# Softmax exponentials in mid phase, first-tile convolution terms summed on VectorE, conversions gated by their own loads

## The chip, the cores and the metric

One core of one Trainium2 chip runs the kernel as one program. The metric is device microseconds of one execution, lower is better. TensorE (PE) does the matmuls, VectorE (DVE) and ScalarE (ACT) the elementwise work, SyncE's queue (SP) issues the DMAs, and GpSimd (POOL) does almost nothing.

## What is computed

A causal convolution of 7 taps with softmax weights per head, then two feed-forward layers, in fp32, over 2 x 4096 tokens of 192 channels.

```
w = softmax(weight_gen, axis=-1)            # [2, 4096, 8 heads, 7 taps]
out[s, h, :] = sum_k w[s, h, k] * x_pad[s + k, h, :]     # 6 rows of zeros ahead, 24 channels a head
x = out.reshape(8192, 192)
x = (silu(x @ w_gate) * (x @ w_val)) @ w_out             # moe:  192 -> 1536 -> 192
h = x @ w_in                                             # moe2: 192 -> 2048 -> 192
result = (h * clip(h + 3, 0, 6) / 6) @ w_out2
```

## The kernel before

**Tiles and phases.** The 8192 tokens are 16 tiles of 512. A tile goes through the convolution, the first layer M1 (phase (1,t), 12 blocks of 128 of the 1536 columns) and the second layer M2 (phase (2,t), 8 blocks of a pair of 128 columns each). Tiles 0 and 1 go through M1 interleaved, as `START` says (so many blocks of tile 0, then so many of tile 1 and tile 0 by turns). Then come phases (1,2), (1,3), and from there (2,t) and (1,t+3) alternate.

**A product in fp32.** Every operand is split into a rounded high part (fp32r, a Copy on ScalarE) and the rest (a subtraction on VectorE), and a product is three passes on TensorE over half heights of 64 rows (L604, L763, L685). An M1 block is: projections pg and pv (L604), Silu on ScalarE (L638), product (L641, DVE), high part gh (L617, ACT), low part gl (L646, DVE), output matmuls (L685). An M2 block is: two projections ph (L604, 18 records), two Relu with bias 3 (L724, ACT), min and product (L728, DVE), gh (L617), gl (L736), output matmuls (L763). The `ph` tiles sit in four PSUM buffers, so the projections of block k+2 need the L728 of block k. In TensorE's order the 12 last matmuls of one block's projections and the 6 first of the next can stand side by side, with output matmuls behind them.

**Boundaries between layers.** At the start of (2,t) the sums of M1 are split on ScalarE and VectorE into M2's operand (L702, L703, L704, L705, L659, L660); this chain is named y below. M2's output matmuls (L763) write PSUM banks that the chain reads, so they wait for it.

**The convolution.** Softmax weights are made for two tiles at a time in items: peak (L325), subtraction (L328), Exp on ScalarE (L329), total (L332), L336, reciprocal (L337), scale (L340). Exp and Silu lie in different function tables of ScalarE, so each change costs an ACT_TABLE_LOAD; Relu and Copy need none. From tile 2 on, taps (L360) and their sums (L385) run on VectorE. For tiles 0 and 1 each of the 7 taps (`conv_pe_items`) goes as a product on VectorE (`tmp`, L360) and as a term of transposing matmuls on TensorE (L421, 16 records in the trace), which adds up the 7 terms in PSUM; `transposes` then has the sum split (L469, L471 on ACT, L475, L477 on DVE). `heat` issues matmuls of no use between (L452).

**Weights.** The weights come as 64-bit words (raw) and are taken apart into fp32 by an exponent on ScalarE (L212), three steps on VectorE (L218, L221, L227), and the split (L278, L296 on ACT, L263 on DVE).

**What sets the order.** The order on each engine is planned when the program is built: `V["A"]` and `V["D"]` are modelled times of ScalarE and VectorE, `fill` takes items of the convolution (queue c) and of the weights (queue w) with a due block (`dues`) into gaps. ScalarE's work that items ask for goes into `late_act`, and `run_act` issues it when the model has room; `urgent` holds the splits that the next phase needs.

Of the kernel before, what the change touches and what calls it, by code (L numbers as in the profile page):

```python
# [38 lines left out]
def conv_swiglu_relu6_kernel(  # L39
# [11 lines left out]
    nc = tc.nc  # L51
# [19 lines left out]
    START = [(0, 6), (6, 10), (10, 12)]  # L71
# [52 lines left out]
    def load_x(t):  # L124
# [12 lines left out]
        def before():  # L137
            for b in range(B):
                r0 = (b * PB + 1) * J - z
                nc.sync.dma_start(  # L140
                    out=xt[b * PB + 1:(b + 1) * PB, :z, :],
                    in_=xf[r0:r0 + (PB - 1) * J, :].rearrange("(p j) d -> p j d", j=J)[:, :z, :],
                )
# [5 lines left out]
    late_act, late_pe, urgent = [], [], []  # L149
# [18 lines left out]

    def run_urgent():
        run_act()  # L170
        while urgent:
            f, a, d, ready = urgent.pop(0)
            f()
            on("A", a, ready)
            on("D", d, ready + min(a, 700.0))

# [6 lines left out]
    def load_raw(limit):  # L183
        while loaded[0] < min(limit, len(chunks)):
# [13 lines left out]
    def convert_stream(q0, q1):  # L198
# [9 lines left out]
        def exponent(q):  # L208
# [6 lines left out]
            late_act.append((gates["e", q], go, chunks[q][0] + 110, V["D"]))  # L215
# [90 lines left out]
    def softmax_items(t0, t1):  # L306
# [97 lines left out]
    def conv_pe_items(t):  # L404

        n = sizes[t]

        def tap(k):
            def go():
                src = vp if k % 2 else pools["c"]  # L410
                o = src.tile([P, MJ, D], F32, tag="tmp", name="tmp", bufs=2)
                taps(nc.vector, t, k, o)
                if k == 0:
                    after_taps(t)

                def pe():
                    if k == PAD:
                        pe_t[t] = [acc_bank(0), acc_bank(2)[:D2]]
                    for dst, a, b in zip(pe_t[t], (0, P), (P, D)):
                        for s in range(n):  # L420
                            nc.tensor.matmul(  # L421
                                dst[:, s * P:(s + 1) * P], o[:, s, a:b], ident,
                                start=k == PAD and s == 0, stop=k == 0 and s == n - 1,
                            )
                late_pe.append((pe, V["D"]))
            return go

        return [(v_cost(n * D), tap(k)) for k in range(PAD, -1, -1)]
# [25 lines left out]
    def run_pe(limit=None):  # L454
        while late_pe and (limit is None or late_pe[0][1] <= limit):
            f, ready = late_pe.pop(0)
            f()
            clock[:] = [max(clock + [ready]) + 1150] * 2

    def transposes(t, banks=None):  # L460
# [5 lines left out]
        if t in pe_t:  # L466
# [5 lines left out]
            late_act.append(([False], rounds, 1850, max(clock) + 300))  # L472

            def lower():
                nc.vector.tensor_sub(s0[:, 1, :N], ba, s0[:, 0, :N].bitcast(F32))  # L475
                for r in HALVES:
                    nc.vector.tensor_sub(s2[r, 1, :N], bb, s2[r, 0, :N].bitcast(F32))  # L477
                x_at[t] = max(V["D"] + 1900, V["A"])
            urgent.append((lower, 0, 1900, max(clock) + 600))
# [35 lines left out]
        late_act.append(([False], rounds, 1300, max(clock) + 600))  # L515

        def lower():
            for v, h, l in parts:
# [5 lines left out]
            x_at[t] = V["D"] + 4500  # L524
        urgent.append((lower, 0, 1500, max(clock) + 800))
# [191 lines left out]
    def m2_ew(b, t, i, ps, there):  # L717
# [15 lines left out]
        at = [on("A", 635, a) for a in at]  # L733
        fill(at[0], at[1] + 1000)
# [97 lines left out]
    def pop(q):  # L832
        at = ready(q)
        if at is None:
            run_act()
            at = ready(q)
# [173 lines left out]
    dues["c", 1] = START[0][1]  # L1010
# [20 lines left out]
    with tc.manual_schedule():  # L1031
# [13 lines left out]
        load_raw(2)  # L1045
        load_x(1)()
        load_raw(4)
        load_wg(1)
# [10 lines left out]
        first = taps0[:1] + s1[:2] + taps0[1:2] + s1[2:] + taps0[2:]  # L1059
# [72 lines left out]
```

## Time and profile before

| | |
|---|---|
| time, median of 3 runs | 1294.22 us (1293.24 to 1295.1) |
| profiled execution | 1291.2 us, its span 1289.3 us |
| TensorE busy | 1259.3 us, 98% of the span |
| VectorE busy | 918.3 us, 71% |
| ScalarE busy | 679.5 us, 53% |
| mean granted TensorE clock | 0.991 of full speed |

The span is the time between the first and the last instruction of the trace; 1.9 us of the execution lie around it. A matmul that waits within the array or runs at a lower clock counts as busy.

### The profile page before, as it was taken

How to read it: one execution, taken by the hardware profiler on the slowest of the kernel's cores; microseconds unless marked ns; L12 is line 12 of the kernel's file. 1: busy time of each engine (PE TensorE's matmuls, PEld its weight loads, DVE VectorE, ACT ScalarE, POOL GpSimd, SP SyncE). 2: the span in 40 equal slices, each digit the busy share in tenths (PEclk: the TensorE clock that was granted, in tenths of full speed). 3: DMA queues.
4: the chain of work that ended last, by engine and by line, in shares of the span. 5: the costliest groups of instructions: out<-in, count | busy, mean ns of one | idle time of the engine just before them, and what ended most of it. 6: DMA issues, size and time to landing. Idle time of an engine off the chain costs nothing.

```text
span 1289.3 us, 29299 instructions
## 1 busy us (share of the span) xinstructions
PE 1259.3 (98%) x12176; PEld 1178.2 (91%) x12176; DVE 918.3 (71%) x1469; ACT 679.5 (53%) x1177; POOL 3.6 (0%) x11
## 2 busy tenths in 40 slices
PE   9889999999999999999999999999999999999998
PEld 7667978898899998999988999889989999999997
DVE  6779986887685947768586775859568594655665
ACT  3355564664554645555464545545455463645655
POOL 1000000000000000000000000000000000000000
PEclk9999999999999999999999999999999999999999
DMA  8312240011010100101001010010100000000000
GB/s 243 122 32 88 60 128 3 10 52 52 17 45 9 48 14 17 44 18 51 10 10 44 18 51 10 9 44 18 44 18 14 10 10 14 18 13 10 13 14 13
DMA packets 26580, 46.95 MB, mean 36 GB/s; under 512 B 3028, under 2 KB 19410, under 8 KB 26448
## 3 DMA queue, kind: packets, MB, share of 16 engines
q1 hardware_dynamic: 26448, 45.09, 12.0%
q8 instruction: 95, 1.56, 0.5%
q14 instruction: 37, 0.30, 0.1%
HBM read 30.92 MB, written 6.29 MB: 29 GB/s over the span
## 4 chain that ended last, share of the span: by engine, by line
PE 80%; DVE 9%; ACT 4%; issue 1%; DMA 0%; SPq 0%; ACTq 0%; DVEq 0%
PE a L763 21%; PE ph L604 19%; PE pv L604 14%; PE a L685 13%; PE pg L604 12%; DVE p L641 2%; ACT gh L617 1%; DVE gl L646 1%; DVE p L728 1%; ACT p L638 1%; DVE s L704 0%; ACT s L659 0%; DVE y L705 0%; DVE tmp L360 0%; DVE f L221 0%
## 5 line engine op out<-in xcount | busy, mean ns | idle before, releaser
L604 PE MATMUL pv<-s,wi 64*128 64x512 f32 x1728 | 449.0, 395 | 5.1 <-ACT p L638 3.8
L604 PE MATMUL pg<-s,wi 64*128 64x512 f32 x1728 | 427.6, 395 | 4.0 <-DVE wi L263 1.3
L617 ACT ACTIVATE gh<-p 128x512 fp32r<-128x512 f32 x448 | 279.0, 633 | 203.7 <-DVE p L641 161.1
L604 PE MATMUL ph<-s,wi 64*128 64x512 f32 x2304 | 330.1, 397 | 9.8 <-DVE p L728 9.1
L604 PEld LDWEIGHTS pv<-s,wi 64*128 64x128 f32 x1728 | 308.8, 184 | 26.6 <-ACT p L638 4.7
L763 PE MATMUL a<-wo,gh 64*128 64x384 f32 x2016 | 318.8, 357 | 1.4 <-DVE y L705 1.0
L604 PEld LDWEIGHTS pg<-s,wi 64*128 64x128 f32 x1728 | 297.8, 185 | 20.6 <-DVE wi L263 2.2
L763 PE MATMUL a<-wo,gl 64*128 64x192 f32 x2016 | 304.7, 250 | 0.0
L763 PEld LDWEIGHTS a<-wo,gh 64*128 64x128 f32 x2016 | 284.5, 187 | 6.0 <-DVE y L705 2.5
L604 PEld LDWEIGHTS ph<-s,wi 64*128 64x128 f32 x2304 | 263.6, 185 | 24.1 <-DVE p L728 14.7
L763 PEld LDWEIGHTS a<-wo,gl 64*128 64x128 f32 x2016 | 280.6, 190 | 0.1
L685 PE MATMUL a<-gh,wo 64*128 64x512 f32 x1152 | 254.9, 393 | 2.2 <-ACT wo L296 2.1
L724 ACT ACTIVATE p<-ph,three 128x512 f32<-128x512 f32 x256 | 162.2, 686 | 162.9 <-PE ph L604 162.6
L641 DVE TENSOR_TENSOR p<-p,pv 128x512 f32<-128x512 f32 x192 | 131.7, 686 | 131.4 <-ACT p L638 130.7
L685 PE MATMUL a<-gl,wo 64*128 64x512 f32 x768 | 212.3, 393 | 0.0
L728 DVE SCALAR_TENSOR_TENSOR p<-p,ph 128x512 f32<-128x512 f32 x256 | 164.0, 682 | 60.2 <-ACT p L724 59.9
L646 DVE TENSOR_TENSOR gl<-p,gh 128x512 fp32r<-128x512 f32 x192 | 132.7, 691 | 104.1 <-ACT gh L617 104.1
L638 ACT ACTIVATE p<-pg 128x512 f32<-128x512 f32 x192 | 114.7, 597 | 168.0 <-PE pg L604 141.7
L685 PEld LDWEIGHTS a<-gh,wo 64*128 64x128 f32 x1152 | 170.8, 184 | 12.3 <-ACT wo L296 2.6
L736 DVE TENSOR_TENSOR gl<-p,gh 128x512 fp32r<-128x512 f32 x256 | 165.6, 689 | 13.0
L685 PEld LDWEIGHTS a<-gl,wo 64*128 64x128 f32 x768 | 121.0, 185 | 6.2
L360 DVE TENSOR_TENSOR tmp<-xt,wg 128x768 f32<-128x768 f32 x98 | 92.5, 953 | 2.3 <-DMA xt<-in_x_dram 1.4
(65 smaller groups left out, 517.3 us busy)
## 6 DMA issues: line engine op xcount, KB each, us to landing
xt<-in_x_dram SPq DMA_DIRECT2D x14, 960.0 KB, 4.8
out_dram<-o SPq DMA_DIRECT2D x15, 384.0 KB, 2.3
s<-s SPq DMA_DIRECT2D x16, 256.0 KB, 2.8
s<-s SPq DMA_DIRECT2D x56, 64.0 KB, 2.0
raw<-in_moe_w_out_dram SPq DMA_DIRECT2D x8, 384.0 KB, 3.1
raw<-in_moe_w_out_dram SPq DMA_DIRECT2D x3, 768.0 KB
raw<-in_moe_w_in_dram SPq DMA_DIRECT2D x16, 128.0 KB, 2.3
wg<-in_weight_gen_dram SPq DMA_DIRECT2D x7, 224.0 KB, 5.0
```

Of the source, the lines that this page charges most:

```text
L360: eng.tensor_mul(o.rearrange("p j (h g) -> p j h g", h=H), xt_t[t][:, a + k:b + k, :].rearrange("p j (h g) -> p j h g", h=H), wg_t[t][:, a ...
L604: return nc.tensor.matmul(ps[b][:, :N], w[rows, s, m, c], x[rows, l, :N], start=start, stop=stop)
L617: nc.scalar.activation(gh[:, :N], p[:, :N], AF.Copy)
L638: nc.scalar.activation(p[:, :N], pg[:, :N], AF.Silu)
L641: nc.vector.tensor_mul(p[:, :N], p[:, :N], pv[:, :N])
L646: nc.vector.tensor_sub(gl[:, :N], p[:, :N], gh[:, :N].bitcast(F32))
L685: return nc.tensor.matmul(y[:, :N], wo1[rows, i, col:col + P], x[rows, :N], start=start, stop=stop)
L724: nc.scalar.activation(q, ph[:, :N], AF.Relu, bias=three)
L728: nc.vector.scalar_tensor_tensor(out=q, in0=q, scalar=6.0, in1=ph[:, :N], op0=ALU.min, op1=ALU.mult)
L736: nc.vector.tensor_sub(gl[:, :N], q, gh[:, :N].bitcast(F32))
L763: return nc.tensor.matmul(z[s][:, :w], x[rows, s * P:(s + 1) * P], late["wo2"][rows, blk, :w], start=start, stop=stop,)
```

## The change

Seven edits:

- **Exp.** The softmax's Exp goes into a list of its own, `late_exp`, which `run_exp` issues. In M2 it is called from the third block of a phase on. For tiles 2 and 3 peak, subtraction and Exp move ahead of the first Silu.
- **Terms.** `TERMS` groups the taps of tiles 0 and 1: taps of one group are added on VectorE (L440 of the changed kernel), and each group is one term on TensorE: 5 terms for tile 0 and 4 for tile 1, instead of 7 and 7.
- **START** goes from (0,6), (6,10), (10,12) to (0,4), (4,8), (8,12).
- **Loads.** `land["w", q]` gives a conversion its own load's modelled time. The second part of tile 0's x comes in 4 DMAs instead of 2, and the second load of softmax weights (`load_wg(1)`) stands ahead of tile 1's x.
- **Transposes.** The ACT half of the split of a tile's convolution (`rounds`) stands with its DVE half in `urgent`; `run_urgent` no longer calls `run_act` first.
- **Dues** of the softmax items of tiles 1 to 3 and the model's cost of a term (2100 for 1150).
- **End.** The last two blocks' output matmuls of the last tile: the first block's for all four strips of 128 tokens, and then the last block's strip by strip, instead of both blocks' strip by strip.

```diff
-    START = [(0, 6), (6, 10), (10, 12)]
+    TERMS = [[[6], [5], [4], [3, 2], [1, 0]], [[6, 5], [4, 3], [2, 1], [0]]]
+    START = [(0, 4), (4, 8), (8, 12)]
...
-            for b in range(B):
+            cuts = [z, z // 2, 0] if t == 0 else [z, 0]
+            for hi, lo in zip(cuts, cuts[1:]):
+                for b in range(B):
...
+    def run_exp():
+        while late_exp:
+            gate, f, ready = late_exp.pop(0)
+            f()
+            gate[0] = on("A", 1900, ready)
+
     def run_urgent():
-        run_act()
         while urgent:
...
+            land["w", q] = V["D"] + 5500
...
-            late_act.append((gates["e", q], go, chunks[q][0] + 110, V["D"]))
+            late_act.append((gates["e", q], go, chunks[q][0] + 110, max(V["D"], land["w", q])))
...
-            late_act.append((gate, lambda: nc.scalar.activation(w(), w(), AF.Exp), 3100, V["D"]))
+            late_exp.append((gate, lambda: nc.scalar.activation(w(), w(), AF.Exp), V["D"]))
...
+        def add():
+            o = box["tmp"][:, :n, :]
+            nc.vector.tensor_add(o, o, box["acc"][:, :n, :])
...
+        for q, term in enumerate(TERMS[t]):
+            items.append((c, step(term[0], "tmp")))
+            for k in term[1:]:
+                items += [(c, step(k, "acc")), (c, add)]
...
-            late_act.append(([False], rounds, 1850, max(clock) + 300))
 
             def lower():
+                rounds()
...
         at = [on("A", 635, a) for a in at]
+        if i >= 2:
+            run_exp()
         fill(at[0], at[1] + 1000)
...
+        for i, g in rest[:-1]:
+            for s in range(sizes[t]):
+                m2_out_last(t, i, g, s)
         for s in range(sizes[t]):
-            for i, g in rest:
-                m2_out_last(t, i, g, s)
+            m2_out_last(t, *rest[-1], s)
             m2_evacuate(t, s, za_t[t][s], o)
             nc.sync.dma_start(out=ov[:, starts[t] + s, :], in_=o[:, s, :])
...
-        load_wg(1)
```

On ScalarE at the start of phase (2,2) before, the first rows are block 0's Relu and gh, then the Exp with its table load, the y chain, and block 1:

```order
L724 ACTIVATE p<-ph,three 128x512 x2
L617 ACTIVATE gh<-p 128x512 x2
L329 ACT_TABLE_LOAD
L329 ACTIVATE wg_1792<-wg_1792 128x448
L702 ACTIVATE s_4485<-a_3973 128x512
L703 ACTIVATE y_4494<-a_3974 64x512
L659 ACTIVATE s_4486<-y_4494 64x512
```

The same place in the changed kernel (L762 is the Relu, L655 gh, L740, L741 and L697 the y chain, L342 the Exp):

```order
L762 ACTIVATE p<-ph,three 128x512 x2
L655 ACTIVATE gh<-p 128x512 x2
L740 ACTIVATE s_4452<-a_3940 128x512
L741 ACTIVATE y_4460<-a_3941 64x512
L697 ACTIVATE s_4453<-y_4460 64x512
L762 ACTIVATE p<-ph,three 128x512 x2
L655 ACTIVATE gh<-p 128x512 x2
L762 ACTIVATE p<-ph,three 128x512 x2
L655 ACTIVATE gh<-p 128x512 x2
L342 ACT_TABLE_LOAD
L342 ACTIVATE wg_1723<-wg_1723 128x448
```

The y chain now follows block 0 directly, and Exp with its load stands behind block 2's gh. On VectorE the softmax's next steps stand behind that block too: the rows there in the changed kernel are block 2's min and product (L766) and gl (L776), the softmax (L345, L349, L350), and block 3:

```order
L766 SCALAR_TENSOR_TENSOR p<-p,ph 128x512 x2
L776 TENSOR_TENSOR gl<-p,gh 128x512 x2
L345 TENSOR_REDUCE sm_4615<-wg_1723 128x64
L349 TENSOR_SCALAR sm_4615<-sm_4615 128x64
L350 RECIPROCAL sm_4615<-sm_4615 128x64
L766 SCALAR_TENSOR_TENSOR p<-p,ph 128x512 x2
```

Total, L349 and reciprocal stand ahead of block 3's L766; the scale follows later.

VectorE in the first tile before: taps of tile 0 (xt_105), with conversion steps of the first weights between the fifth and the sixth tap:

```order
L360 TENSOR_TENSOR tmp<-xt_105,wg_103 128x768 x3
L218 TENSOR_SCALAR f_224<-f_224 128x384
L221 SCALAR_TENSOR_TENSOR f_224<-raw_112,f_224 128x384
L227 SCALAR_TENSOR_TENSOR f_224<-raw_112,f_224 128x384
L360 TENSOR_TENSOR tmp<-xt_105,wg_103 128x768 x2
```

and in the changed kernel:

```order
L373 TENSOR_TENSOR tmp<-xt_105,wg_103 128x768 x3
L373 TENSOR_TENSOR acc<-xt_105,wg_103 128x768
L440 TENSOR_TENSOR tmp<-tmp,acc 128x768
L373 TENSOR_TENSOR tmp<-xt_105,wg_103 128x768
L373 TENSOR_TENSOR acc<-xt_105,wg_103 128x768
L440 TENSOR_TENSOR tmp<-tmp,acc 128x768
L231 TENSOR_SCALAR f_201<-f_201 128x384
```

The taps now stand side by side, with two sums (L440), and the conversions (L231 is L218 of before) come behind the last of them.

## Rows read from the trace of the kernel before

**Rows 1.** The page's busy time of each engine.

```profile
PE 1259.3 (98%) x12176; PEld 1178.2 (91%) x12176; DVE 918.3 (71%) x1469; ACT 679.5 (53%) x1177; POOL 3.6 (0%) x11
```

**Rows 2.** Waits of PE: line, releaser; total us, times, longest us.

```profile
PE ph L604 <- DVE p L728: 9.1, 7, 1.3
```

**Rows 3.** Timeline of ACT, start of (2,2): start, us, engine, line, operation, [idle before].

```profile
336.37 1.27 ACT L724 ACTIVATE p<-ph,three 128x512 f32<-128x512 f32 x2 [1.05 <-PE ph L604]
...
339.11 1.28 ACT L329 ACT_TABLE_LOAD   x1
340.40 0.58 ACT L329 ACTIVATE wg<-wg 128x448 f32<-128x448 f32 x1
...
343.49 1.27 ACT L724 ACTIVATE p<-ph,three 128x512 f32<-128x512 f32 x2
346.82 1.23 ACT L617 ACTIVATE gh<-p 128x512 fp32r<-128x512 f32 x2 [2.06 <-DVE p L728]
...
353.75 1.27 ACT L724 ACTIVATE p<-ph,three 128x512 f32<-128x512 f32 x2 [3.12 <-PE ph L604]
```

**Rows 4.** Timeline of PE, same place.

```profile
346.85 2.85 PE L604 MATMUL ph<-s,wi 64*128 64x512 f32 x12 [1.31 <-DVE p L728]
```

**Rows 5.** Windows: us, busy us of PE, PEld, DVE, ACT, POOL; granted clock; DMA.

```profile
336.37:353.75 17.38, 15.73 (x138) 13.87 (x136) 13.05 (x22) 10.95 (x17) 0.00 (x0) 0.90 0.07 16
415.55:428.26 12.71, 12.71 (x137) 12.63 (x135) 11.68 (x19) 9.10 (x16) 0.00 (x0) 1.00 0.10 22
490.06:507.43 17.37, 15.72 (x139) 13.92 (x136) 13.05 (x22) 10.96 (x18) 0.00 (x0) 0.90 0.08 17
221.44:237.26 15.82, 14.18 (x138) 12.00 (x136) 12.99 (x22) 10.96 (x18) 0.00 (x0) 1.00 0.08 18
```

**Rows 6.** Timeline of ACT, blocks 2 and 3 of (2,3).

```profile
425.47 1.23 ACT L617 ACTIVATE gh<-p 128x512 fp32r<-128x512 f32 x2 [0.20 <-DVE p L728]
428.26 1.27 ACT L724 ACTIVATE p<-ph,three 128x512 f32<-128x512 f32 x2 [1.55 <-PE ph L604]
```

**Rows 7.** Timeline of DVE: softmax steps of (2,2), then (2,3).

```profile
344.11 0.60 DVE L332 TENSOR_REDUCE sm<-wg 128x64 f32<-128x448 f32 x1
...
344.98 0.55 DVE L337 RECIPROCAL sm<-sm 128x64 f32<-128x64 f32 x1
...
428.22 0.95 DVE L385 TENSOR_TENSOR acc<-acc,tmp 128x768 f32<-128x768 f32 x1
429.09 1.28 DVE L728 SCALAR_TENSOR_TENSOR p<-p,ph 128x512 f32<-128x512 f32 x2
```

**Rows 8.** Timeline of PE in (2,3), then in (2,1).

```profile
431.64 2.27 PE L604 MATMUL ph<-s,wi 64*128 64x512 f32 x17
...
277.95 1.80 PE L604 MATMUL ph<-s,wi 64*128 64x512 f32 x9 [1.19 <-DVE p L728]
```

**Rows 9.** Timeline of PE at the end, tile 15's last two blocks.

```profile
1280.83 0.44 PE L778 MATMUL a<-wo,gh 128*128 128x384 f32 x1 [1.49 <-ACT gh L617]
...
1282.63 0.37 PE L778 MATMUL a<-wo,gh 128*128 128x384 f32 x1
...
1285.53 0.37 PE L778 MATMUL a<-wo,gh 128*128 128x384 f32 x1
```

**Rows 10.** Windows of the first tiles, columns as in rows 5.

```profile
0.00:107.92 107.92, 97.00 (x696) 76.48 (x698) 80.25 (x124) 45.40 (x69) 3.61 (x11) 0.97 0.43 124
107.92:218.40 110.48, 107.68 (x919) 90.65 (x917) 92.74 (x166) 60.37 (x113) 0.00 (x0) 1.00 0.26 76
```

**Rows 11.** Timeline of PE, tile 0's terms.

```profile
9.66 12.79 PE L421 MATMUL a<-ident,tmp 128*128 128x128 f32 x96 [0.34 <-DVE tmp L360]
```

**Rows 12.** Timeline of DVE and ACT in the first tiles.

```profile
25.16 0.96 DVE L360 TENSOR_TENSOR tmp<-xt,wg 128x768 f32<-128x768 f32 x1
...
94.34 0.36 DVE L218 TENSOR_SCALAR f<-f 128x384 int32<-128x384 int32 x1 [4.69 <-ACT f L212]
...
93.77 0.54 ACT L212 ACTIVATE f<-raw 128x384 f32<-128x384 f32 x1 [4.92 <-DMA raw<-in_moe_w_in_dram]
```

More of the change, by code (lines that the diff above doesn't have):

```diff
@@ L406, in conv_pe_items, with step @@
         n = sizes[t]
-        def tap(k):
+        box, count, items = {}, [0], []
+        c = v_cost(n * D)
+        def step(k, tag):
             def go():
[L410 to L413, printed above, removed]
-                    after_taps(t)
[L416 to L425, printed above, removed]
-            return go
@@ L428, in conv_pe_items @@
-        return [(v_cost(n * D), tap(k)) for k in range(PAD, -1, -1)]
+                if tag == "acc":
+                    o = vp.tile([P, MJ, D], F32, tag="acc", name="acc", bufs=1)
+                else:
+                    count[0] += 1
+                    src = vp if count[0] % 2 else pools["c"]
+                    o = src.tile([P, MJ, D], F32, tag="tmp", name="tmp", bufs=2)
+                box[tag] = o
+                taps(nc.vector, t, k, o[:, :n, :])
+                if k == TERMS[t][-1][-1]:
+                    after_taps(t)
@@ new lines, in step, with pe, go @@
+            return go
+        def add():
+            o = box["tmp"][:, :n, :]
+            nc.vector.tensor_add(o, o, box["acc"][:, :n, :])
+        def pe(first, last):
+            o = box["tmp"]
+            def go():
+                if first:
+                    pe_t[t] = [acc_bank(0), acc_bank(2)[:D2]]
+                for dst, a, b in zip(pe_t[t], (0, P), (P, D)):
+                    for s in range(n):
+                        nc.tensor.matmul(
+                            dst[:, s * P:(s + 1) * P], o[:, s, a:b], ident,
+                            start=first and s == 0, stop=last and s == n - 1,
+                        )
+            late_pe.append((go, V["D"]))
@@ L431, in conv_swiglu_relu6_kernel, with both @@
+        for q, term in enumerate(TERMS[t]):
+            items.append((c, step(term[0], "tmp")))
+            for k in term[1:]:
+                items += [(c, step(k, "acc")), (c, add)]
+            _, f = items.pop()
+            def both(f=f, first=q == 0, last=q == len(TERMS[t]) - 1):
+                f()
+                pe(first, last)
+            items.append((c, both))
+        return items
     free = list(range(4))
@@ L477, in lower @@
                     nc.vector.tensor_sub(s2[r, 1, :N], bb, s2[r, 0, :N].bitcast(F32))
-                x_at[t] = max(V["D"] + 1900, V["A"])
-            urgent.append((lower, 0, 1900, max(clock) + 600))
+                return lambda: x_at.update({t: V["D"]})
+            urgent.append((lower, 1850, 1900, max(clock) + 300))
             return
@@ L1058, in conv_swiglu_relu6_kernel @@
         s1 = [(("c", -1), x[0], x[1], x[2] if len(x) > 2 else None) for x in s1]
-        first = taps0[:1] + s1[:2] + taps0[1:2] + s1[2:] + taps0[2:]
+        s2 = [(("c", -2), x[0], x[1], x[2] if len(x) > 2 else None) for x in s2]
+        first = taps0[:1] + s1[:2] + taps0[1:]
         queues["c"] += first
```

56 lines of the change are left out of this document (34 added, 22 removed).

## The prediction, made before the changed kernel ran

> **What bounds the kernel now.** I read the page's busy times first. TensorE is busy 1259.3 of 1289.3 us [rows 1], so time can be won only where it idles, runs at a lower clock, or does work that can go. The waits of TensorE come next: the largest is projections ph on VectorE's L728, seven times, 9.1 us [rows 2]. Six of the seven lie at the start of the phases (2,0), (2,2), ... (2,10), and the seventh in (2,1).
>
> At (2,2) ScalarE runs block 0's Relu at 336.37, the table load at 339.11, Exp at 340.40, the y chain, and block 1's Relu at 343.49 only [rows 3]. L728 of block 1 is late by as much, and the projections of block 3 wait 1.31 for it until 346.85 [rows 4]. The reader should then compare windows from block 0's Relu to block 3's: 17.38 us at (2,2), granted clock 0.90, against 12.71 at (2,3), clock 1.00, where no Exp stands [rows 5]. Of the 4.67 between them 1.65 is idle time of TensorE (17.38 less 15.73). The other 3.02 is matmuls that take longer: PE's x138 need 15.73 at the one and x137 need 12.71 at the other. So the clock falls to its lower level, 1.2 GHz, for a part of the window, behind the wait. (2,4) has 17.37. (2,0) has 15.82 with clock 1.00 [rows 5].
>
> The start is different: up to the product of the 16th block (107.92 us) VectorE is busy 80.25 and TensorE's clock is 0.97; in the next 110.48 us TensorE is busy 107.68 [rows 10]. In the first stretch neither engine is full: they wait for each other.
>
> **Exp in mid phase.** The y chain follows block 0 at once, as in the phases without Exp. I take the whole difference: five boundaries of 17.38 - 12.71 = 4.67, 23.3 us, and (2,0) with 15.82 - 12.71 = 3.11, together **26.4**. Lower bound: at (2,0) 1.64 (the idle time alone), 25.0.
>
> What it costs at its new place. Block 2's gh ends at 425.47 + 1.23 = 426.70, and block 3's Relu starts at 428.26 after 1.55 idle [rows 6]. From table load to the end of Exp it is 340.40 + 0.58 - 339.11 = 1.87 [rows 3], so Exp ends at 428.57 and the Relu is 0.31 late. Queued behind it on VectorE are total, L336 and reciprocal, 344.98 + 0.55 - 344.11 = 1.42 [rows 7], ahead of block 3's L728. That starts at about 430.0 instead of 429.09, and its first half ends at 430.7. TensorE needs it for block 5's projections. In the row of 17 at 431.64 the first five or six belong to block 4; at 2.27 / 17 = 0.13 each block 5 starts near 432.3 [rows 8]. The margin is 1.6 us, so I cost the place at nothing. With the cover gone it is up to 4.67 for each of six phases.
>
> The row shows Exp starting 1.29 us after the load's start, with no gap [rows 3]. The Trainium skill (ScalarE: Activation LUTs, What ACT_TABLE_LOAD costs) states a load of about 1283 ns and a drain of about 1380 ns, 2.66 us for each change of set. The load agrees with 1.28; of the drain the row shows nothing. By that page of the Trainium skill the margin would be 0.2 us and not 1.6, and the sum the same as long as nothing else is late.
>
> **Transposes and run_urgent.** The seventh wait, 1.19 in (2,1) [rows 8], is at tile 4's transposes, whose split now comes one block later. I leave it as it is: 0, bounds -1.2 to +1.2.
>
> **The end.** TensorE waits 1.49 at 1280.83 for the last block's gh, with all but one strip of the block before still to do [rows 9]. Ten pairs of matmuls take 1285.53 - 1282.63 = 2.90, 0.29 a pair, and a block's strip is two pairs, 0.58. Three strips, 1.74 us, now stand in front of the wait; 0.28 of a second wait on gl follows it today, so 1.49 + 0.28 hold them. Gain **1.7**. The last four evacuations come at 0.58 each instead of 1.16; if ScalarE, VectorE or the output DMAs don't keep that pace, 0.5 is left.
>
> **The start.** TensorE's terms of tile 0 are 96 records in 12.79 us, 16 to a term, 2.13 each [rows 11].
>
> - Tile 0: two terms fewer, 4.26. VectorE has two adds more, of the form of L385, 0.95 each [rows 7], 1.90. A conversion of 768 columns now stands on ScalarE ahead of the split, about 0.9 (an estimate from 0.54 for 384 [rows 12]). Gain 1.5; from 0 (adds eat it) to 4.26.
> - Tile 1: three terms fewer between the blocks, 6.39, and three adds more, 2.85. Gain 3.5; from 0 to 6.39.
> - ScalarE stands 4.92 at the first w_in conversion, whose load has not landed, in front of a Silu, and VectorE 4.69 behind it [rows 12]. With the load's own time in the model it stands later. Gain 4.7.
> - Given back: conversion steps and one sum that were done ahead of the 16th product (two L218 of 0.36, two of some 0.55, one of 0.95) come later, 2.8. VectorE has 110.48 - 92.74 = 17.7 us free in the next stretch, but TensorE only 2.8 [rows 10]. I take the whole 2.8.
>
> The sum is 1.5 + 3.5 + 4.7 - 2.8 = **7**; bounds 2 (the w_in wait alone) and 12.5. As a check: VectorE's work up to the 16th product grows by five adds less those items, 4.75 - 2.8 = 2, to 82; at 107.9 - 9.7 = 98 it would be busy 84% of the time. That is high, and the reason that the lower bound stays in play.
>
> Costed at nothing: the Exp of tiles 2 and 3 at the start (0.58, under TensorE's terms; 0.58 if it isn't hidden), the cut load of x (the same bytes in four issues of SP), and tile 1's x behind the second load of weights. Tile 1's first tap ran at 25.16 [rows 12], and now stands behind the third product, so its load has longer. If it is late, tile 1 is, by the length of one load.
>
> **The sum.** 26.4 + 1.7 + 7 = 35.1 against the profiled execution's 1291.2 (span 1289.3) gives 1256.1. The median of the runs, 1294.22, is 3.0 above that execution, so I predict **1259** for a median. Its own range is 1252 to 1266: the start's bounds, -5.5 and +5, and a microsecond or two for (2,0) and the runs.
>
> **Rivals.**
>
> - *Exp in mid phase stalls TensorE too.* For it: ScalarE is already 0.31 late by the rows, VectorE has a sum and a tap in that gap (L385 at 428.22 just ahead of L728 [rows 7]), and the margin of 1.6 hangs on all of them. Against: after one block the 1.55 idle takes the lateness up. A stall of 1 us at six places gives 1265; with the clock falling as at the boundary, 4.67 each, it is near 1285. Chance 0.10. The drain that the Trainium skill states (ScalarE: Activation LUTs, What ACT_TABLE_LOAD costs) would put it at the edge of stalling.
> - *The start wins nothing.* VectorE sets the pace there, five adds cost 4.75, tile 1 is needed two blocks earlier than before, and the conversions for the blocks move together with it. Without gain 1266; with the adds on the path 1271. For it: 84% busy. Against: 27.7 us idle today, of which 4.69 is one wait. Chance 0.18.
> - *The boundary keeps its low clock.* If the y chain itself brings the clock down, only the idle time goes: six times 1.65, 10, for 26.4, which gives 1275. Against: (2,3) has the same chain at clock 1.00. Chance 0.06.
> - *Slower: the low clock holds through the first tiles.* If TensorE, with 10.6 us less to do for the terms (9 of 2.13 instead of 14) and VectorE as the bound, idles a little in each block, its clock can stay at 1.2 GHz. Then half of each such stretch is lost, at most. It has to last for twice 35 us before the gain is gone and some 75 us before the kernel is slower; the stretch up to (2,0) at 221.44 [rows 5] offers some 190. Against: today's waits there leave the clock at 0.97 on average, some 3% [rows 10]. At 80 us it would be 1299. Chance 0.03.
>
> **How the numbers follow.** My forecast has 0.63. The range of 8 in 10 reaches from 1248 to 1272: all of the forecast's own range, the start without gain, and a mid-phase stall of up to 2 us. It leaves out the low clock at the boundaries (0.06), the slower case (0.03), the worse half of the stalls (0.05) and ends of the rest. A measurement of this kernel tells 0.2%, 2.6 us, from no change. Every rival but the last is faster by more: faster 0.95. Slower has 0.03, and between them lies 0.02.
>
> **What the profile would show.** Right: ACT_TABLE_LOAD after block 2's gh in (2,even), from the Relu of block 0 to that of block 3 12.7 us there at clock 1.00, and no wait of ph on L728 but perhaps in (2,1); the 16th M1 product near 98 us; no wait of several us for w_in's raw; at the end no wait on gh. Wrong: a wait of ph on L728 in the fifth block behind Exp; a windows row there with a clock under 1; in the first 110 us VectorE's share over 85% and TensorE's clock well below 0.97.

## The result, and the profile after

The changed kernel takes 1254.76 us (median of 4 runs, 1253.16 to 1255.15), the kernel before 1294.66 us in the same comparison (1293.24 to 1297.77). The ratio is 0.9686, 95% interval 0.9667 to 0.9706. The profiled execution of the changed kernel took 1254.63 us with a span of 1252.7, 36.6 less than the span of before.

Where the 36.6 us came from, by the starts of the same blocks' Relus in the two traces: 8.9 up to phase (2,0) (221.44 before, 212.56 after), 3.1 from there to (2,2), 23.0 in the five phase pairs from (2,2) to (2,12), nothing from there to tile 15, and 1.7 at the end. The 8.9 of the start hang on the two profiles that are compared; the first experiment shows by how much.

The page's busy times and the waits of TensorE after the change (line, releaser: total us, times, longest us):

```profile
PE 1232.9 (98%) x12096; PEld 1185.4 (95%) x12096; DVE 920.4 (73%) x1474; ACT 675.4 (54%) x1175; POOL 3.6 (0%) x11
```

```profile
PE a L450 <- DVE tmp L440: 3.7, 1, 3.7
PE pg L642 <- ACT s L507: 2.9, 1, 2.9
PE a L723 <- ACT wo L309: 2.3, 1, 2.3
...
PE ph L642 <- DVE p L766: 0.8, 1, 0.8
```

Of the seven waits of projections on min and product [rows 2] one is left, the one in (2,1). The first three rows here all lie in the first 46 us.

ScalarE at the start of (2,2), where rows 3 stood (L762 is Relu, L740 and L697 the y chain, L342 Exp):

```profile
324.40 1.27 ACT L762 ACTIVATE p<-ph,three 128x512 f32<-128x512 f32 x2 [1.05 <-PE ph L642]
...
327.69 0.60 ACT L740 ACTIVATE s<-a 128x512 fp32r<-128x512 f32 x1 [0.56 <-PE a L723]
...
330.31 1.27 ACT L762 ACTIVATE p<-ph,three 128x512 f32<-128x512 f32 x2
...
335.59 1.28 ACT L342 ACT_TABLE_LOAD   x1
336.88 0.58 ACT L342 ACTIVATE wg<-wg 128x448 f32<-128x448 f32 x1
337.37 1.25 ACT L762 ACTIVATE p<-ph,three 128x512 f32<-128x512 f32 x2
339.51 1.22 ACT L655 ACTIVATE gh<-p 128x512 fp32r<-128x512 f32 x2 [0.89 <-DVE p L766]
341.45 1.27 ACT L762 ACTIVATE p<-ph,three 128x512 f32<-128x512 f32 x2 [0.72 <-PE ph L642]
```

The y chain follows block 0 at once, and block 1's Relu starts 5.9 us behind block 0's instead of 7.1 [rows 3]. Exp stands behind block 2, and block 3's Relu follows it without a gap. Block 4's Relu waits for TensorE again (0.72), so ScalarE has caught up within one block. The same windows as in rows 5 and 10:

```profile
324.40:337.37 12.97, 12.97 (x139) 12.97 (x138) 10.37 (x17) 10.98 (x18) 0.00 (x0) 1.00 0.10 22
...
212.56:225.49 12.93, 12.93 (x139) 11.93 (x137) 10.37 (x17) 10.98 (x18) 0.00 (x0) 1.00 0.10 22
0.00:98.57 98.57, 86.59 (x615) 67.81 (x617) 81.57 (x123) 40.61 (x64) 3.61 (x11) 0.93 0.41 120
98.57:209.52 110.95, 107.67 (x919) 86.29 (x917) 94.94 (x170) 60.77 (x116) 0.00 (x0) 1.00 0.31 90
```

TensorE is busy for the whole of 12.97 us at full clock, against 15.73 of 17.38 at 0.90 [rows 5]. The 16th product of M1 starts at 98.57 instead of 107.92, and VectorE is busy 81.57 up to there (83%). The granted clock in this first stretch is lower than before, 0.93.

The end, tile 15's last block on TensorE, for rows 9:

```profile
1246.05 0.36 PE L818 MATMUL a<-wo,gh 128*128 128x384 f32 x1
1246.60 0.36 PE L819 MATMUL a<-wo,gl 128*128 128x192 f32 x1 [0.19 <-DVE gl L776]
...
1249.05 0.25 PE L819 MATMUL a<-wo,gl 128*128 128x192 f32 x1
```

The wait of 1.49 for gh is gone. From block 3's Relu of tile 15 to the last matmul it is 1249.05 - 1226.30 = 22.75, before it was 1285.74 - 1261.26 = 24.48: 1.73 less.

### The profile page after: what moved, and what is told of

It is laid out like the page before. It is cut to its first block, busy times and chain, and to the rows that moved or that the text cites. A ratio compares the mean times of both kernels' runs of the same rounds, so it can differ in the third digit from the quotient of the medians.

```text
span 1252.7 us, 29336 instructions
## 1 busy us (share of the span) xinstructions
PE 1232.9 (98%) x12096; PEld 1185.4 (95%) x12096; DVE 920.4 (73%) x1474; ACT 675.4 (54%) x1175; POOL 3.6 (0%) x11
## 4 chain that ended last, share of the span: by engine, by line
PE 89%; DVE 6%; ACT 2%; issue 1%; DMA 0%; DVEq 0%; ACTq 0%; SPq 0%
PE ph L642 22%; PE a L803 22%; PE a L723 16%; PE pv L642 15%; PE pg L642 13%; DVE p L679 1%; DVE gl L684 1%; PE a L450 1%; DVE f L234 1%; ACT gh L655 1%; DVE f L240 0%; DVE wi L276 0%; DVE acc L398 0%; DVE f L231 0%; DVE tmp L373 0%
## 5 line engine op out<-in xcount | busy, mean ns | idle before, releaser
L642 PE MATMUL pg<-s,wi 64*128 64x512 f32 x1728 | 455.4, 397 | 5.7 <-ACT s L507 2.9
L642 PE MATMUL pv<-s,wi 64*128 64x512 f32 x1728 | 425.7, 397 | 2.0 <-DVE p L679 1.2
L655 ACT ACTIVATE gh<-p 128x512 fp32r<-128x512 f32 x448 | 278.9, 633 | 215.0 <-DVE p L679 162.7
L642 PEld LDWEIGHTS pg<-s,wi 64*128 64x128 f32 x1728 | 310.2, 185 | 20.4 <-ACT s L507 3.1
L642 PE MATMUL ph<-s,wi 64*128 64x512 f32 x2304 | 316.6, 393 | 0.9 <-DVE p L766 0.8
L642 PEld LDWEIGHTS pv<-s,wi 64*128 64x128 f32 x1728 | 299.5, 186 | 15.1 <-DVE p L679 2.4
L803 PE MATMUL a<-wo,gh 64*128 64x384 f32 x2016 | 307.9, 353 | 0.0
L803 PE MATMUL a<-wo,gl 64*128 64x192 f32 x2016 | 297.6, 248 | 0.0
L803 PEld LDWEIGHTS a<-wo,gh 64*128 64x128 f32 x2016 | 289.4, 184 | 0.3
L803 PEld LDWEIGHTS a<-wo,gl 64*128 64x128 f32 x2016 | 287.2, 187 | 0.1
L723 PE MATMUL a<-gh,wo 64*128 64x512 f32 x1152 | 253.8, 392 | 2.4 <-ACT wo L309 2.3
L762 ACT ACTIVATE p<-ph,three 128x512 f32<-128x512 f32 x256 | 162.1, 685 | 126.5 <-PE ph L642 125.9
L723 PE MATMUL a<-gl,wo 64*128 64x512 f32 x768 | 208.7, 392 | 0.0
L766 DVE SCALAR_TENSOR_TENSOR p<-p,ph 128x512 f32<-128x512 f32 x256 | 163.5, 680 | 46.3 <-ACT p L762 45.8
L776 DVE TENSOR_TENSOR gl<-p,gh 128x512 fp32r<-128x512 f32 x256 | 165.6, 688 | 13.0
L723 PEld LDWEIGHTS a<-gh,wo 64*128 64x128 f32 x1152 | 163.2, 184 | 10.4 <-ACT wo L309 2.7
L723 PEld LDWEIGHTS a<-gl,wo 64*128 64x128 f32 x768 | 116.8, 184 | 4.2
```

Source lines behind the costliest of these rows:

```text
L642: return nc.tensor.matmul(ps[b][:, :N], w[rows, s, m, c], x[rows, l, :N], start=start, stop=stop)
L655: nc.scalar.activation(gh[:, :N], p[:, :N], AF.Copy)
L723: return nc.tensor.matmul(y[:, :N], wo1[rows, i, col:col + P], x[rows, :N], start=start, stop=stop)
L762: nc.scalar.activation(q, ph[:, :N], AF.Relu, bias=three)
L766: nc.vector.scalar_tensor_tensor(out=q, in0=q, scalar=6.0, in1=ph[:, :N], op0=ALU.min, op1=ALU.mult)
L776: nc.vector.tensor_sub(gl[:, :N], q, gh[:, :N].bitcast(F32))
```

## The experiments

### The kernel before, once more

No edit.

> The kernel before, unchanged, profiled once more: its profiled execution (1291.2 us) lay 3.0 us under the median of its timed runs, and the sum of the prediction was made against it. If the 3 us are windows of the lower clock that come and go, this profile has a span between 1289 and 1294 us, the same steps from block to block as before everywhere else, and any difference lies in whole windows with a granted clock under 1. If the offset belongs to profiling, the span is 1289.3 within 0.5 us.

Span 1292.1, 2.8 more than in the first profile, so the offset does not belong to profiling. Windows of this run, columns as in rows 5:

```profile
224.07:241.44 17.37, 15.72 (x138) 13.36 (x135) 13.06 (x22) 10.95 (x18) 0.00 (x0) 0.90 0.07 16
342.12:357.91 15.79, 14.13 (x137) 12.43 (x135) 12.96 (x22) 10.96 (x18) 0.00 (x0) 1.00 0.08 18
```

The first is (2,0), the second (2,2). In the first profile it was the other way round: (2,0) took 15.82 at clock 1.00 and (2,2) 17.38 at 0.90 [rows 5]. (2,4) has no low clock in this run either, 15.79; (2,6), (2,8) and (2,10) have it. The wait of ph on L728 is the same in both runs, 9.1 us in all. So the stall costs 15.8 - 12.7 = 3.1 us at each of the six boundaries, and the low clock behind it 1.6 more at some: 5 of 6 in one run, 4 of 6 in the other. Seven timed runs of this kernel beside the experiments lie between 1290.47 and 1297.23 us; those of the changed kernel within 2 us.

The 2.8 us do not come from these windows: from (2,0) to the end the two profiles take 1067.9 and 1068.0. They come from the start, where (2,0) begins at 221.44 and at 224.07, so the expectation's "whole windows with a granted clock under 1" is not what the difference is made of. VectorE's wait for the second part of tile 0's x, first profile and then this one:

```profile
8.64 0.96 DVE L360 TENSOR_TENSOR tmp<-xt,wg 128x768 f32<-128x768 f32 x1 [1.41 <-DMA xt<-in_x_dram]
```

```profile
9.60 0.96 DVE L360 TENSOR_TENSOR tmp<-xt,wg 128x768 f32<-128x768 f32 x1 [2.35 <-DMA xt<-in_x_dram]
```

The granted clock from 36 to 46 us is 0.83 in the first profile and 0.66 in this one. At the 16th Silu this one is 2.6 behind.

The start is a draw in the changed kernel too: it comes out differently from one profile of the same code to the next. Three profiles of each start are on record, since three of the runs below leave everything up to (2,0) as it was (ScalarE's and VectorE's rows up to there are the same, in the same order). Times in us:

| | first Silu | 16th Silu | (2,0) |
|---|---|---|---|
| before: first profile, second, Exp alone | 27.90, 28.87, 28.61 | 107.28, 109.86, 109.82 | 221.44, 224.07, 223.93 |
| changed: first profile, Exp back, late Exp | 27.83, 28.43, 27.19 | 97.94, 97.03, 95.81 | 212.56, 211.63, 210.39 |

So the start's gain is 8.9 in the two first profiles and 11.6 between the means, and a run that differs from the changed kernel by a microsecond or two at (2,0) shows nothing yet. From (2,0) on the draws are closer: with no stall at the boundaries, it is 1040.1 to 1040.6 in the changed kernel and in every run below that alters its start, but for the one with START (0,5), 1041.6.

### Exp alone

In the kernel before, the Exp of tiles 4 and later goes into the new list:

```diff
+            if t0 >= 4:
+                late_exp.append((gate, lambda: nc.scalar.activation(w(), w(), AF.Exp), V["D"]))
+                return
...
+        if i >= 2:
+            run_exp()
```

> The kernel before with one part of the change: the Exp of tiles 4 and later goes into the list that is issued from the third block of an M2 phase on. All else is as before. Theory (place of Exp alone): the first (2,0) block's Relu stays at 221.4 us, the span falls by 25 to 26.5 us to 1263 to 1264.5, ratio near 0.980. Rival (the other edits are needed for it, above all that the splits are no longer preceded by ScalarE's late work): less than 20 us.

1267.08 us, ratio 0.9805 (0.9775 to 0.9836), span 1265.3. Phase (2,0) starts at 223.93, as in the second profile of before (224.07), and from there to the end it is 1265.3 - 223.93 = 1041.4 against 1292.1 - 224.07 = 1068.0: 26.7 us less. (2,2) of this run:

```profile
335.74:348.54 12.80, 12.80 (x138) 12.65 (x136) 10.45 (x17) 11.09 (x18) 0.00 (x0) 1.00 0.10 22
```

The place of Exp alone makes the boundaries' gain; the other edits are not needed for it. The theory's span, 1263 to 1264.5, was counted from the first profile's early start; (2,0) did not stay at 221.4.

### Exp back at the boundary

```diff
-        if i >= 2:
+        if i >= 0:
             run_exp()
```

> The changed kernel, but Exp is issued behind block 0's gh again, ahead of the y chain, in the phases (2,0), (2,2) to (2,10). Theory (Exp's place alone makes the boundaries' gain): from block 0's Relu to block 3's 17.4 us at (2,2) to (2,10) and 15.8 at (2,0), clock 0.90 there; span 1252.7 + 26 = 1278 to 1279. Rival (the new way of issuing the splits, or VectorE's other work there, made part of it): the windows stay under 16 us and the span under 1272.

Span 1265.5, 12.8 more than the changed kernel: half of the 26 of the theory, whose windows of 17.4 us and clock of 0.90 are not there. What the rival named is: windows under 16 us and a span under 1272. The window of (2,2), the whole phase pair from (2,2) to (2,3), and TensorE's wait:

```profile
325.80:340.87 15.07, 14.14 (x137) 12.43 (x135) 12.24 (x22) 10.96 (x17) 0.00 (x0) 1.00 0.09 19
325.80:402.68 76.88, 75.95 (x751) 69.09 (x749) 56.08 (x90) 42.07 (x73) 0.00 (x0) 1.00 0.09 26
```

```profile
335.56 2.26 PE L642 MATMUL ph<-s,wi 64*128 64x512 f32 x12 [0.59 <-DVE p L766]
```

All six boundaries take 15.06 to 15.10 us at clock 1.00. Exp delays the y chain as before, but the wait is 0.59 instead of 1.31 [rows 4]. On VectorE the scale of the softmax stands behind block 1's min and product here, and ahead of it in the kernel before; that is 0.62 us of the difference, read from the order in the trace and not tried by itself. With the shorter wait the clock fell at none of the six. Which of the other edits moved the scale was not tried either. So the boundaries' gain against the first profile has three parts: 2.3 us each of Exp's place (76.88 against 74.54 from 324.40 to 398.94 in the changed kernel), 0.7 each of the shorter wait (15.8 - 15.07), and 1.6 at each boundary where the clock fell. From (2,0) to (2,12) it is 883.3 us in the first profile, 871.1 here and 857.2 in the changed kernel. With Exp at the boundary the other edits are worth 12.2 of the 26.1; the run with Exp alone shows that Exp's place is worth all of it without them.

### How late Exp may be

Needless Exps ahead of the real one, 0 to 6 by phase:

```diff
+            def go():
+                for _ in range({6: 1, 8: 2, 10: 3, 12: 4, 14: 6}.get(t0, 0)):
+                    nc.scalar.activation(spare, w(), AF.Exp)
+                nc.scalar.activation(w(), w(), AF.Exp)
```

> The changed kernel with Exp at its new place and needless Exps of 128x448 ahead of it, written to a tile that nothing reads: 0, 1, 2, 3, 4 and 6 of them in the phases (2,0), (2,2), (2,4), (2,6), (2,8), (2,10), 0.49 us each. Theory (Exp has a margin of 1.6 us or a little more, until the projections of block 5 wait): no wait of TensorE on block 3's min and product with 1, 2 and 3 of them (0.5, 1.0, 1.5 us), 0.1 to 0.4 us with 4, 1.1 to 1.4 with 6. Rival (no margin is left, ScalarE's part at the edge): the wait is there with the first and grows by 0.49 with each: 0.5, 1.0, 1.5, 2.0, 2.9.

Each took 0.61 us, not 0.49, so the delays are 0.61, 1.22, 1.83, 2.44 and 3.66. Windows from block 0's Relu of (2,2), (2,4), (2,6), (2,8), (2,10) to that of the next M2 phase; without a dose it is 74.54 (324.40 to 398.94 in the changed kernel):

```profile
322.23:396.80 74.57, 74.57 (x751) 74.37 (x750) 55.79 (x90) 42.50 (x73) 0.00 (x0) 1.00 0.09 27
471.33:546.07 74.74, 74.74 (x751) 69.61 (x750) 55.69 (x90) 42.51 (x75) 0.00 (x0) 1.00 0.09 27
620.67:696.02 75.35, 75.26 (x751) 68.61 (x750) 55.70 (x90) 43.08 (x76) 0.00 (x0) 1.00 0.09 27
770.62:846.56 75.94, 75.41 (x751) 68.55 (x749) 55.69 (x90) 43.67 (x77) 0.00 (x0) 1.00 0.09 27
921.09:999.76 78.67, 76.86 (x751) 75.06 (x750) 55.87 (x90) 45.34 (x78) 0.00 (x0) 0.98 0.05 13
```

and TensorE's waits of the last two:

```profile
788.16 2.24 PE L646 MATMUL ph<-s,wi 64*128 64x512 f32 x12 [0.43 <-DVE p L770]
...
939.88 3.07 PE L646 MATMUL ph<-s,wi 64*128 64x512 f32 x12 [1.72 <-DVE p L770]
```

The loss is 0.0, 0.2, 0.8, 1.4 and 4.1 us. Behind the first us it grows as the dose does: 1.83 costs 0.8 and 2.44 costs 1.4. So the margin is 1.0 us. It exists, and is smaller than predicted. The trace shows why. At (2,6), behind three needless Exps, block 3's L770 ends its first half at 637.56 and its second at 638.15. One matmul of projections starts between the two, at 637.61, and the next only at 638.20, 0.6 us later than its place without a dose. So TensorE needs the second half one matmul after the first. In the last row the clock fell as well, behind a wait of 1.72, and 3.66 - 1.0 = 2.6 became 4.1.

The Trainium skill (ScalarE: Activation LUTs, What ACT_TABLE_LOAD costs) adds a drain of about 1380 ns to each load. The changed kernel shows no such time: block 2's gh ends at 335.57, the load starts at 335.59, and Exp starts 336.88 - 335.59 = 1.29 us behind it. (2,2) with Exp and (2,3) without both last 74.5 us.

### Terms of tiles 0 and 1, one tap each

```diff
-    TERMS = [[[6], [5], [4], [3, 2], [1, 0]], [[6, 5], [4, 3], [2, 1], [0]]]
+    TERMS = [[[6], [5], [4], [3], [2], [1], [0]], [[6], [5], [4], [3], [2], [1], [0]]]
```

> The changed kernel with each tap of tiles 0 and 1 as a term of its own again, 7 and 7 (no sums on VectorE, 10 terms' worth of... five more terms on TensorE than the changed kernel, 2.13 us each, 10.6 us; five adds of 0.95, 4.8 us, less on VectorE). The order START stays (0,4), (4,8), (8,12). Theory of the prediction (TensorE's terms are on the path): phase (2,0) starts about 5 us later than in the changed kernel (212.6), at 217 to 218, the time is 1259 to 1260. Rival (VectorE sets the pace of the first tiles): the sums cost more than the terms, (2,0) starts at 208 to 212 and the time is under 1254.

1257.12 us (1256.3 to 1257.37), ratio to before 0.9716 (0.969 to 0.9742). (2,0) starts at 215.26, 2.7 later than in the changed kernel. The time is 2.4 longer, and (2,0) comes later than in any of the three profiles of the changed start (210.39 to 212.56). So the terms are on the path; the theory's 5 us and 1259 to 1260 are too much by the time. How the gain divides between the tiles is less clear. The first Silu, 28.49, is at the edge of the three draws (27.19 to 28.43). From the first Silu to tile 1's first, the fifth, it is 34.77 us against 31.20 to 32.72, and the last step of it, from the fourth, where tile 1's terms lie, is 20.06 against 18.91 to 18.94: 1.1 us that are clear of the draws.

### Conversions without their load's time

```diff
-            late_act.append((gates["e", q], go, chunks[q][0] + 110, max(V["D"], land["w", q])))
+            late_act.append((gates["e", q], go, chunks[q][0] + 110, V["D"]))
```

> The changed kernel without the conversions' own load times in the model, so that the exponents of w_in's first words are issued earlier in ScalarE's order. Theory: ScalarE stands 4 to 5 us at the first of them again, in front of a Silu, and (2,0) starts 4 to 5 us later, at 217; time 1259. Rival (the wait is made up, since VectorE has less to do behind it): under 1.5 us.

1256.82 us (1255.06 to 1258.43), ratio 0.971 (0.9679 to 0.9741). ScalarE at the first w_in conversion:

```profile
102.74 0.55 ACT L225 ACTIVATE f<-raw 128x384 f32<-128x384 f32 x1 [3.62 <-DMA raw<-in_moe_w_in_dram]
103.71 0.58 ACT L676 ACTIVATE p<-pg 128x512 f32<-128x512 f32 x1
```

ScalarE stands 3.6 us again, in front of a Silu, and (2,0) starts at 216.56, 4.0 later in the profile, 0.6 of which was there at the 16th block. From the 16th Silu to (2,0) it is 118.04 against 114.58 to 114.62 in the three draws, so the wait and what follows it cost 3.4. The time says 2.1, not the theory's 4 to 5; the wait is the one that it named, at a smaller size.

### The order of the first blocks

START as before, (0,6), (6,10), (10,12):

```diff
-    START = [(0, 4), (4, 8), (8, 12)]
+    START = [(0, 6), (6, 10), (10, 12)]
```

> The changed kernel with START as before, (0,6), (6,10), (10,12). In the changed kernel 18.9 us lie between the fourth Silu and the fifth, in which tile 1's taps run and TensorE waits. Theory (two more blocks of tile 0 fill this): the gap falls below 13 us and (2,0) starts 2 to 4 us earlier, time 1251 to 1253. Rival (VectorE bounds the stretch: the two blocks bring their conversions and products ahead of the taps): no gain, (2,0) within 1 us of 212.6 or later by up to 3.

1254.04 us (1251.23 to 1255.16), ratio 0.969 (0.9662 to 0.9718); (2,0) starts at 211.82. The gap falls to 14.8 us (54.57 to 69.37), but the two blocks in front of it take what it gives back: at the 16th block this run is 1.1 us behind the changed kernel's profile, and (2,0) lies among the draws. START is worth nothing that these runs can tell.

With (0,5), (5,9), (9,12):

> The changed kernel with START (0,5), (5,9), (9,12), one block of tile 0 more ahead of tile 1. The two theories are those of the run with START as before, with half of each size: (2,0) 1 to 2 us earlier if the block fills the gap, within 1 us or up to 1.5 later if VectorE bounds it.

1257.93 us (1255.28 to 1258.89), ratio 0.972 (0.9692 to 0.9748); (2,0) starts at 214.87. This is outside both theories. At the tenth Silu it is 1.5 us behind the run with (0,6) (81.17 and 79.68), at (2,0) 3.1. Why it is worse than its neighbours on either side stays open.

### The Exp of tiles 2 and 3

Left where it was in the order of items, but in the new list:

```diff
-        queues["c"][:0] = s2[:2]
-        pop("c")
-        pop("c")
...
-        queues["c"] += s2[2:]
+        queues["c"] += s2
```

> The changed kernel, but peak, subtraction and Exp of tiles 2 and 3 stay behind the first Silu, as before the change, so that ScalarE loads the Exp table and the Silu table once more within M1. The prediction costed this part at nothing. Theory from the trace after the change (it is a part of the start's gain): ScalarE's 1.28 + 0.58 + 1.28 = 3.1 us stand in front of a Silu, (2,0) starts at 214.5 to 216 instead of 212.6, time 1257 to 1258. Rival (hidden, as costed): within 1 us of 212.6.

1274.21 us, ratio 0.9847 (0.9829 to 0.9865), 19.5 more than the changed kernel. TensorE's waits of this run:

```profile
PE b L527 <- DVE sum L403: 18.5, 1, 18.5
```

Up to the 22nd block it runs beside the changed kernel (117.70 and 117.48); then TensorE stands 18.5 us for tile 2's convolution. Within M1 `run_exp` is called only when an item is taken that can't go on without it, so this Exp came at 121.53, its subtraction having ended at 60.30, and tile 2's taps all came behind it. The run does not answer the question; it shows that a list that M1 empties only at need wants this Exp ahead of M1.

The same with this one Exp in the list of before:

```diff
+            if t0 == 2:
+                late_act.append((gate, lambda: nc.scalar.activation(w(), w(), AF.Exp), 3100, V["D"]))
+                return
```

> As the run with the Exp of tiles 2 and 3 within M1, but this one Exp is issued at once, when its subtraction is done, as before the change, so that tile 2's taps are not held back to the end. Theory (18.5 us of that run were tile 2's late sum, and not the table loads): no wait of TensorE on tile 2's sum over 1 us; the two loads and Exp, 3.1 us, stand in front of a Silu, and (2,0) starts 2 to 6 us later than in the changed kernel (212.6), at 214.5 to 218.5, time 1257 to 1261. Rival (the place of this Exp costs nothing, as the prediction had it): (2,0) within 1 us of 212.6, time within 1.5 us of 1254.8.

1270.1 us (1268.61 to 1270.86), ratio 0.9818; (2,0) starts at 227.97, 15.4 later, far outside both theories. ScalarE and TensorE in this run:

```profile
72.57 1.28 ACT L343 ACT_TABLE_LOAD   x1
73.87 0.58 ACT L343 ACTIVATE wg<-wg 128x448 f32<-128x448 f32 x1
74.35 0.83 ACT L291 ACTIVATE wi<-f 128x768 fp32r<-128x768 f32 x1
```

```profile
75.23 0.79 PE L645 MATMUL pg<-s,wi 64*128 64x512 f32 x1 [4.75 <-ACT wi L291]
...
89.59 0.79 PE L645 MATMUL pg<-s,wi 64*128 64x512 f32 x1 [4.63 <-ACT wi L291]
```

Its subtraction ended at 59.35, and Exp started at 73.87. `late_act` is first in, first out, and issues its head only when the model finds room for it, here for 3.1 us. For 13 us there was none, though ScalarE and VectorE idled between Silus and products, and the conversion of the next weights (L291) came right behind Exp. TensorE then waited 4.75 and 4.63 for those weights. By these rows it is not the 3.1 us of loads on ScalarE that cost most, but what came behind Exp in the list. That is read from the order and the waits; no run let the conversions pass. (In the kernel before the subtraction ended at 79.37 and Exp's load started 0.9 us later, at 80.26, in another order of blocks.)

### The hole in front of the first projections

22 more matmuls of no use behind tile 0's terms:

```diff
-    HEAT = [14, 6]
+    HEAT = [14, 28]
```

> The changed kernel with 28 instead of 6 matmuls of no use behind tile 0's terms, 2.9 us more of them, which fill TensorE's wait for the split (18.7 to 21.7 us in the changed kernel). Theory (the shorter chain of terms left a hole, the clock fell behind it for some 7 us, and this took the gain of tile 0's terms): granted clock 1.00 from 20 to 29 us, first Silu at 25 to 26.5 instead of 27.8, (2,0) 1 to 2 us earlier. Rival (the conversions set the pace behind it): the first Silu earlier, the third and (2,0) as in the changed kernel within 0.5 us.

1256.65 us (1254.49 to 1257.15). The window 20 to 29 us, first of the changed kernel, then of this one:

```profile
20.00:29.00 9.00, 7.01 (x28) 4.63 (x30) 6.72 (x11) 7.00 (x11) 0.00 (x0) 0.63 1.04 310
```

```profile
20.00:29.00 9.00, 8.78 (x73) 7.18 (x73) 7.37 (x13) 6.30 (x11) 0.00 (x0) 1.00 1.04 323
```

The clock is at full speed and the first Silu 0.7 us earlier (27.14). The third starts at 36.81 for 36.92, as the rival said, behind a wait of TensorE for weights (L723 on ScalarE's wo) that grew from 2.28 to 2.65. The fourth is 0.8 earlier again, and so is every one up to the 36th. (2,0) starts at 213.65, 1.1 later than in the changed kernel's profile, outside the rival's 0.5. All of that loss comes between the 36th and the 39th Silu, where TensorE waits for a transfer; the same wait is 0.18 in the changed kernel:

```profile
169.72 0.49 PE L642 MATMUL pg<-s,wi 64*128 64x512 f32 x1 [2.01 <-DMA s<-s]
```

Neither the theory's 1 to 2 us at (2,0) nor a better time is seen. In this pair of profiles the low clock from 20 to 29 us costs 0.8 us up to there, less than the draws differ by.

ScalarE's split of tile 0 ahead of the conversion that waits for its load:

```diff
-        run_act()
         queues["c"][:0] = s2[:2]
...
         run_urgent()
+        run_act()
         run_exp()
```

> The changed kernel, but ScalarE's split of tile 0 is issued ahead of the exponent of the third load of weights, whose landing it now stands behind until 19.8 us. Theory (this in-order wait, 3.4 us, took the gain of tile 0's terms): the split starts at 17.3 to 18 instead of 21.0, the first projections at 18 to 19 instead of 21.7, the first Silu at 24 to 25.5 instead of 27.8, and (2,0) 1 to 3 us earlier, time 1252 to 1254. Rival (the weights behind it set the pace): the third Silu stays at 36 to 37 and (2,0) within 1 us.

ScalarE in the changed kernel, and then in this run:

```profile
19.82 0.89 ACT L225 ACTIVATE f<-raw 128x768 f32<-128x768 f32 x1 [3.36 <-DMA raw<-in_moe_w_val_dram]
20.61 0.51 ACT L291 ACTIVATE wi<-f 128x384 fp32r<-128x384 f32 x1
21.03 0.58 ACT L507 ACTIVATE s<-a 128x512 fp32r<-128x512 f32 x1
```

```profile
16.85 0.60 ACT L507 ACTIVATE s<-a 128x512 fp32r<-128x512 f32 x1 [0.40 <-PE a L450]
17.87 1.20 ACT L509 ACTIVATE s<-a 64x512 fp32r<-64x512 f32 x2 [0.42 <-PE a L450]
19.53 0.90 ACT L225 ACTIVATE f<-raw 128x768 f32<-128x768 f32 x1 [0.46 <-DMA raw<-in_moe_w_val_dram]
```

The split starts 4.2 us earlier and the first Silu 2.9 (24.90). The third Silu is 1.0 earlier, tile 1's first and all from there to the 40th 2.5, (2,0) 0.95. The 1.5 were lost between the 40th and the 41st: TensorE's wait of 1.0 there is the same in both runs, but behind it the granted clock fell in this one (0.79 from 180 to 188 us). The time is 1253.69 us (1253.04 to 1254.31), 1.07 below the changed kernel, less than these runs can tell, and the earliest of the three draws has its 16th Silu at 95.81, this run at 95.46. So a gain in time is not shown. The first Silu, 2.3 ahead of the earliest draw, shows where tile 0's terms went in the changed kernel: the split waited, in order, behind a conversion whose load had not landed.

## Why the prediction was right, and where its steps were off

**The boundaries: 26.4 forecast, 26.1 measured.** The first profile of before gave 4.67 for five and 3.11 for one, and the changed kernel took all of it back. Exp alone did the same (26.7 against the second profile). The reading of the parts failed: "the other 3.02 is matmuls that take longer", put down to the clock, was 1.4 us of longer busy time at full clock, as a stalled matmul counts as busy (14.13 in the second profile's (2,2) against 12.71), and 1.6 us of low clock. The row of (2,0) in rows 5 had it: busy 14.18 against 12.71, at clock 1.00. And the 1.6 is not part of a boundary; it came at 5 of 6 in one run and at 4 of 6 in the next.

**Exp in mid phase: costed at nothing, and it costs nothing.** Its margin was given as 1.6 us and is 1.0. Block 3's Relu, min and product came as computed: min and product start 14.45 us behind block 0's Relu (338.85 - 324.40), which is the forecast's 430.0 - 415.55. The step that was off is which half block 5's projections need: it took the first, and the second, 0.6 later, is needed at nearly the same time. The rival of a stall there did not come true; it stood 1.0 us away.

**The end: 1.7 forecast, 1.73 measured.** The transposes in (2,1): 0 forecast, and the wait there went from 1.19 [rows 8] to 0.8; in the run with Exp back at the boundary it is 1.2 again.

**The start: 7 forecast, 8.9 measured in the first profiles and 11.6 between the means of three, from parts of other sizes.** By the start of the k-th Silu in the two first profiles, the changed kernel is ahead by 0.1 us at the first, 3.0 at the seventh, 3.1 at the ninth, 4.8 at the eleventh, 9.4 at the twelfth, 9.3 at the sixteenth, and 8.9 at (2,0).

- Tile 0: 1.5 forecast, 0.1 seen (0.6 between the means). The estimate had the conversion's 0.9 in front of the split, not its wait for the load:

```profile
21.66 0.49 PE L642 MATMUL pg<-s,wi 64*128 64x512 f32 x1 [2.94 <-ACT s L507]
...
45.35 10.06 PE L450 MATMUL a<-ident,tmp 128*128 128x128 f32 x64 [3.75 <-DVE tmp L440]
```

  TensorE, done with its terms, waited 2.94 us for the split, and the clock fell behind it (0.63 from 20 to 29 us). With the split ahead the first Silu gains 2.9 us; two thirds of them are gone at the third Silu, which waits for the weights.
- The cut load of x, costed at nothing, stands in the same stretch: VectorE's wait for x's second part, 1.41 to 2.35 us in the profiles of before, is 0 to 0.53 in those of the changed start. No run undid this edit, so its share of the gain stays open.
- Tile 1: 3.5 forecast, 2.9 seen between the first and the seventh Silu (4.6 between the means; 2.0 to 3.6 came back when the terms of both tiles were undone). The second row above is the other side of it: TensorE waits 3.75 for the first sum and then runs the four terms in 10.06 us, of which four times 2.13 would be 8.5; the granted clock was 0.83 there.
- w_in's conversion: 4.7 forecast, 4.6 seen between the eleventh and the twelfth Silu. Undone, 2.1 us in time, 3.4 behind the 16th Silu in the profile.
- The Exp of tiles 2 and 3: costed at nothing, 1.7 seen between the ninth and the eleventh Silu, in all three profiles of either start. The forecast priced its new place and left out what the old one cost. Put back in the changed order of blocks it cost 14 to 15 us (one run), more than its 3.1 us on ScalarE, by what came behind it in a list that issues in order.
- Given back: 2.8 forecast, 0.5 seen. That VectorE's free 17.7 us took the rest fits; it was not tried.

These parts don't add up from the single undoings (2.7, 4.0, -0.7 and 15.4 at (2,0) for terms, loads, START and Exp, each with a draw's 2 us or so in it).

**The median.** The sum said 1256.1 for the profiled execution, which took 1254.63. The 3.0 that I added, since the profile of before lay that much under its median, was not there after: the profiled execution lies at the median. The second profile of before shows where such an offset comes from: its start is 2.6 later, and the rest is the same. The first profile had an early start, so the start's gain was counted short against it. Between the medians the change is worth 1294.66 - 1254.76 = 39.9 us, of which the forecast's 35.1 leaves 4.8 out; the start, 7 forecast and 11.6 between the means, holds nearly all of that. That 1259 came within 4.2 us is the boundaries' and the end's doing; the start's sum was low.

**The rivals.** VectorE as the bound of the start was right about the engine (it is busy 83% up to the 16th product) and wrong about the gain: its idle time fell by 10.7 us, and the adds take 4.75. A low clock through the first tiles came in part, 0.93 for 0.97 (0.93 to 0.95 in the three profiles of the changed start, 0.94 to 0.97 in those of before). Of its cost, the run with more matmuls tried one stretch only.

## What to carry to other kernels

Work that blocks an in-order engine for two microseconds belongs where the next engine has as much in hand, and the slack can be measured by doses of useless work, one per phase, in a single run. An order list that is first in, first out holds back all that stands behind its head: look for who waits for the second entry before the first is costed at its own duration. A profile is one draw, of the waits for the first loads and of the clock behind each stall alike: profile the kernel before twice, take the steady part for the sum, and ask of every experiment whether its difference is larger than that between two profiles of the same code.

## What the runs showed of the hardware that was not expected

With the same instructions in the same order, the granted clock fell to the lower level behind a TensorE wait of 1.3 us at 9 of 12 boundaries in two profiles, and each fall cost 1.6 us (17.37 against 15.79). Behind waits of 0.59 us (six boundaries) and 0.43 us it did not fall, behind one of 1.72 us it did. Behind the wait of 1.0 us near 180 us (182.07 in the changed kernel's profile, 179.57 with the split ahead) it fell in one of these two runs and not in the other. ScalarE's table load cost 1.29 us to the start of the next activation wherever it stood.
